# On-chip transposes for all 21 first slots and hardware-queue weight loads with a GpSimd cast, in a fused attention and feed-forward kernel

## The chip, the cores and the metric

The kernel runs on one core of a Trainium2 chip. The metric is device microseconds of one execution, in the median of several. All runs that are used here are fast. Sizes below about 2% are resolved by repeated rounds in which the kernel under test and the kernel before run on the same chip. A ratio is the mean time of one kernel's fast runs over that of the other's of the same rounds, so it isn't quite the ratio of the medians that are quoted beside it.

## The reference

Attention with a threshold, then a feed-forward layer, all in float32 on the outside:

```python
scores = (q @ k.T) / sqrt(64)                 # 8 batches, 8 heads, 576 tokens, 64 columns
scores = where(scores >= max(scores) - tau, scores, -1e9)
attn   = exp(scores - max(scores)); attn /= sum(attn) + 1e-9
x      = attn @ v                             # heads side by side: (4608, 512)
h      = x @ w_in                             # w_in (512, 2048)
out    = (h * clip(h + 3, 0, 6) / 6) @ w_out  # w_out (2048, 512)
```

## The kernel before

The attention is cut into 144 slots of two 128x576 score tiles each. In one iteration of the main loop the engines work on neighbouring slots: VectorE takes the maxima of slot n, ScalarE the exponentials of slot n-1 and the masks of slot n, TensorE the scores of slot n+1, GpSimd the normalization of slot n-1. GpSimd and SyncE take their instructions in program order in every trace read here (below, at 108.44 us, a small instruction stands behind a cast that waits).

The normalized tile must be transposed for the product with v. Slots up to 20 with an odd number are transposed on TensorE (nine 128x128 transposes into PSUM, one VectorE copy); all others by a DMA transpose that SyncE issues:

```python
sl.on_chip = len(queue) < N1 - 1 and len(queue) % 2 == 1        # N1 = 22
...
def sm_norm(sl):                                                # GpSimd
    for i in range(2):
        nc.gpsimd.tensor_scalar(out=pn[:, i, :], in0=sl.s[:, i, :], scalar1=sl.rinv[:, i:i + 1], ...)
    if not sl.on_chip:
        nc.sync.dma_start_transpose(out=sl.dst, in_=pn)
```

The feed-forward weights arrive as bf16 through 32 casting DMAs of 128x512, which the program issues from GpSimd (the prediction names why). The end of an iteration, which the change edits (cut):

```python
queue[n + 1].tiles = scores(...)       # TensorE
if n < 8:
    warm_up(6)                         # six float32 transposes of the identity, to no purpose but the clock
if prev is not None:
    sm_norm(prev)
flush(); late.extend(outs)
start(loads, 1)                        # q and k, SyncE
if n < 4 or n > 12:
    start(vcasts, 1)                   # v, a casting DMA from GpSimd
if n > 3:
    start(casts, 1 if n < 24 else 2)   # weights, casting DMAs from GpSimd
```

The first product with w_in comes in slot 23, the first with w_out in slot 31. From about there TensorE is the bound.

## Time and profile before

| | before |
|---|---|
| median of the first three runs | 562.35 us |
| profiled span | 562.3 us |
| TensorE, ScalarE, VectorE, GpSimd busy | 95%, 84%, 75%, 54% |
| mask of slots 0, 23 and 31 starts at | 10.7, 82.5 and 112.25 us |

The busy shares are means over two stages: up to slot 31 ScalarE and GpSimd lead, afterwards TensorE. The prediction shows the busy time by stretch. In the lines of a profile PE is TensorE, DVE VectorE, ACT ScalarE and POOL GpSimd; SPq and POOLq are what SyncE and GpSimd do to issue. What else one needs of the profile before are two lines of the page's part on DMA issues (destination and source, issuing queue, count, size, time from issue to landing), where the 32 weight DMAs stand:

```profile
w_in_sb<-in_moe_w_in_dram POOLq DMA_DIRECT2D x16, 128.0 KB, 4.1
w_out_sb<-in_moe_w_out_dram POOLq DMA_DIRECT2D x16, 128.0 KB, 4.5
```

Here are GpSimd and the mask that waits for it in the iteration of slot 28, from the instructions in order of time (start, duration, engine, line and operation, with the idle time before it in brackets):

```profile
98.92 0.80 POOL L121 DMA_DIRECT2D vm<-in_v_dram  x1
99.72 1.07 POOL L146 DMA_DIRECT2D w_out_sb<-in_moe_w_out_dram  x2
100.87 0.46 POOL L280 TENSOR_SCALAR bias<-m 128x1 f32<-128x1 f32 x2
101.08 1.44 ACT L285 ACTIVATE s<-s,bias 128x576 f32<-128x576 f32 x2 [1.39 <-POOL bias L280]
```

GpSimd spends 1.9 us on issuing a v load and two weight loads, and the tiny bias behind them makes ScalarE stand still for 1.39 us. Nobody waits for the data of these DMAs: their destinations lie fixed in memory and are needed slots later.

### The profile page before, as it was taken

To read this page: it belongs to the slowest core of one execution; us is meant where nothing else is said; L and a number is where in the kernel's file an instruction comes from. 1 tells how busy PE (TensorE), PEld (TensorE's weight loads), DVE (VectorE), ACT (ScalarE), POOL (GpSimd) and SP (SyncE) were. 2 spreads that over 40 slices of the span, in tenths; PEclk is the share of its full clock that TensorE was granted. 3 is DMA by queue.
4 is the path that set the end of the run, shared out by engine and by line. 5 is a ranking of instruction groups with operands and counts; after the bars stand their busy time and mean duration, and the time that the engine had idled before them with its cause. 6 is when DMAs were issued, how large, how long until landed. Compare 5 with 4: busy or idle time off the path is not lost.

```text
span 562.3 us, 11634 instructions
## 1 busy us (share of the span) xinstructions
PE 535.0 (95%) x3856; PEld 309.3 (55%) x3856; DVE 424.4 (75%) x1040; ACT 470.3 (84%) x999; POOL 305.2 (54%) x646
## 2 busy tenths in 40 slices
PE   7998798899999999999999999999999999999997
PEld 5665455455545565555555565655555565654663
DVE  3588787687878788787878798887978798883440
ACT  4799899798988999989898999899898999983540
POOL 1678878854556555655456555755556555561000
PEclk8899999899999999999999999999999999999999
DMA  5879999997689876978589867987699865453102
GB/s 110 135 110 166 162 160 184 207 148 144 112 159 153 151 153 127 208 139 155 114 150 170 159 137 146 174 160 146 127 137 175 167 124 117 101 109 86 38 20 75
DMA packets 286204, 77.52 MB, mean 138 GB/s; under 512 B 269248, under 2 KB 281536, under 8 KB 286144
## 3 DMA queue, kind: packets, MB, share of 16 engines
q1 hardware_dynamic: 268736, 67.86, 64.8%
q0 software_dynamic: 17408, 8.92, 13.7%
q8 instruction: 30, 0.49, 0.4%
q14 instruction: 30, 0.25, 0.2%
HBM read 36.70 MB, written 9.44 MB: 82 GB/s over the span
## 4 chain that ended last, share of the span: by engine, by line
PE 58%; DVE 11%; ACT 9%; issue 4%; POOL 1%; DMA 1%; SPq 1%; DVEq 0%; POOLq 0%
PE h L353 18%; PE o L382 17%; PE s L256 16%; DVE s L277 5%; ACT s L285 4%; PE av L323 3%; ACT s L290 3%; DVE g L370 2%; DVE r L364 2%; ACT r L362 2%; PE s L262 1%; PE tp L213 1%; PE ar L323 1%; DVE osb L390 1%; POOL pn L298 1%
## 5 line engine op out<-in xcount | busy, mean ns | idle before, releaser
L298 POOL TENSOR_SCALAR pn<-s,rinv 128x576 bf16<-128x576 f32 x288 | 211.6, 745 | 133.5 <-issue 58.5
L277 DVE TENSOR_SCALAR_CACHE_REDUCE s<-s 128x576 f32<-128x576 f32 x288 | 205.9, 752 | 44.9 <-PE s L256 35.2
L285 ACT ACTIVATE s<-s,bias 128x576 f32<-128x576 f32 x288 | 207.1, 766 | 36.8 <-POOL bias L280 35.7
L290 ACT ACTIVATE s<-s 128x576 f32<-128x576 f32 x288 | 192.7, 671 | 0.3
L256 PE MATMUL s<-kT,qT 64*128 64x288 f32 x1024 | 172.7, 435 | 5.4 <-DVE s L277 3.2
L353 PE MATMUL h<-xT,w_in_sb 128*128 128x320 bf16 (+1 forms) x1024 | 145.0, 287 | 5.5 <-DVE g L370 4.6
L382 PE MATMUL o<-w_out_sb,g 128*128 128x512 bf16 x576 | 140.9, 379 | 3.6 <-DVE osb L390 3.0
L353 PEld LDWEIGHTS <-w_in_sb 128*128 128x128 bf16 x1024 | 92.0, 97 | 68.4 <-issue 31.1
L256 PEld LDWEIGHTS s<-kT,qT 64*128 64x128 f32 x1024 | 94.8, 188 | 62.7 <-DVE s L277 24.9
L370 DVE SCALAR_TENSOR_TENSOR g<-r,h 128x512 bf16<-128x512 f32 (+1 forms) x128 | 96.4, 754 | 41.2 <-ACT r L362 39.3
L280 POOL TENSOR_SCALAR bias<-m 128x1 f32<-128x1 f32 x288 | 54.4, 189 | 69.0 <-DVE s L277 48.2
L382 PEld LDWEIGHTS <-g 128*128 128x128 bf16 x576 | 55.6, 98 | 58.2 <-issue 9.8
L362 ACT ACTIVATE r<-h,three 128x640 f32<-128x640 f32 (+1 forms) x74 | 54.4, 737 | 21.1 <-PE h L353 20.4
L290 ACT ACTIVATION_READ_ACCUMULATOR s<-s 128x1 f32 x288 | 54.2, 188 | 0.0
L364 DVE TENSOR_SCALAR r<-h 128x512 f32<-128x512 f32 (+1 forms) x54 | 40.5, 751 | 0.0
L390 DVE TENSOR_SCALAR osb<-o 128x512 f32<-128x512 f32 x31 | 21.0, 676 | 22.2 <-PE o L382 22.2
L323 PE MATMUL av<-pT,vm 128*64 128x512 bf16 x256 | 34.6, 392 | 2.0 <-ACT kT L203 2.0
L323 PEld LDWEIGHTS <-vm 128*64 128x64 bf16 x512 | 18.1, 111 | 25.2 <-issue 18.3
L293 DVE RECIPROCAL rinv<-rsum 128x2 f32<-128x2 f32 x144 | 23.0, 160 | 10.2 <-ACT s L290 9.5
L335 DVE CAST xT<-av 128x512 bf16<-128x512 f32 x32 | 21.8, 681 | 5.6 <-PE av L326 5.3
L277 DVE DVE_READ_ACCUMULATOR s<-s 128x1 f32 x288 | 23.9, 83 | 0.0
L388 ACT ACTIVATE osb<-o 128x512 f32<-128x512 f32 x5 | 3.0, 597 | 23.9 <-PE o L382 23.9
(42 smaller groups left out, 255.9 us busy)
## 6 DMA issues: line engine op xcount, KB each, us to landing
km<-in_k_dram SPq DMA_DIRECT2D x64, 128.0 KB, 3.0
out_dram<-osb SPq DMA_DIRECT2D x32, 256.0 KB, 2.4
nq<-in_q_dram SPq DMA_DIRECT2D x96, 72.0 KB, 2.7
vm<-in_v_dram POOLq DMA_DIRECT2D x16, 256.0 KB, 5.4
nq<-in_q_dram SPq DMA_DIRECT2D x16, 128.0 KB, 3.9
w_in_sb<-in_moe_w_in_dram POOLq DMA_DIRECT2D x16, 128.0 KB, 4.1
w_out_sb<-in_moe_w_out_dram POOLq DMA_DIRECT2D x16, 128.0 KB, 4.5
pT<-pn SPq DMA_TRANSPOSE x119, 3.4
```

Of the source, the lines that this page charges most:

```text
L256: nc.tensor.matmul(tiles[a][:, hf, 0:HALF], qT_of(pair)[a * 64:(a + 1) * 64, t * P:(t + 1) * P], keys(pair, a, hf), start=True, stop=True)
L277: nc.vector.tensor_scalar(out=sl.s[:, i, :].rearrange("p (a b) -> p a b", a=2), in0=ps[:, :, 0:HALF], scalar1=1.0, scalar2=None, op0=Alu.m ...
L280: nc.gpsimd.tensor_scalar(out=sl.bias[:, i:i + 1], in0=sl.m[:, i:i + 1], scalar1=-scale, scalar2=tau, op0=Alu.mult, op1=Alu.add)
L285: nc.scalar.activation(out=s, in_=s, func=Act.Prelu, bias=sl.bias[:, i:i + 1], scale=scale, alpha=REJECT)
L290: nc.scalar.activation(out=s, in_=s, func=Act.Exp, accum_out=sl.rsum[:, i:i + 1])
L298: nc.gpsimd.tensor_scalar(out=pn[:, i, :], in0=sl.s[:, i, :], scalar1=sl.rinv[:, i:i + 1], scalar2=1.0, op0=Alu.mult, op1=Alu.mult)
L323: nc.tensor.matmul(ps[a * 64:(a + 1) * 64, :], vm[:, 2 * hp + a, c * D:(c + 1) * D], pT[:, 5 * a + c, cols], start=(c == 0), stop=False)
L353: nc.tensor.matmul(hps[:, n, 0:w], w_in_sb[:, ki, (ni + n) * P:(ni + n + 1) * P], xT[b][:, ki, c0:c0 + w], start=(ki == 0), stop=(ki == KI ...
L362: nc.scalar.activation(out=r, in_=hps, func=Act.Relu, bias=three[:])
L364: nc.vector.tensor_scalar(out=r, in0=hps, scalar1=3.0, scalar2=0.0, op0=Alu.add, op1=Alu.max)
L370: nc.vector.scalar_tensor_tensor(out=gbuf[:, ni:ni + 2, c0:c0 + w], in0=r, scalar=6.0, in1=hps, op0=Alu.min, op1=Alu.mult)
L382: nc.tensor.matmul(o_ps[0], gbuf[:, ni, mt * P:(mt + 1) * P], w_out_sb[:, ni, :], start=(ni == 0), stop=(ni == NI - 1))
```

## The change

The intent: transposing all of the first 21 slots on TensorE takes eleven DMA transposes out of the busiest stage and keeps TensorE's clock up with useful work in place of warm-ups; loading the weights as float32 through SyncE's hardware queue frees GpSimd from issuing them and moves longer rows. GpSimd then casts from a staging buffer.

```diff
+    w_pool = ctx.enter_context(tc.tile_pool(name="wp", bufs=3))
...
+        def load(dst, src):
+            st = w_pool.tile([P, 2, 512], F32, tag="w", name="w")
+            nc.sync.dma_start(out=st[:], in_=src)
+            for n in range(2):
+                landed.append((dst[:, n, :], st[:, n, :]))
...  (16 loads of 512 KB in place of 32 casting DMAs)
+    def cast():
+        dst, src = landed.pop(0)
+        nc.gpsimd.tensor_copy(out=dst, in_=src)
...
-            sl.on_chip = len(queue) < N1 - 1 and len(queue) % 2 == 1
+            sl.on_chip = len(queue) < N1 - 1
...
-        if n < 8:
-            warm_up(6)
...
-        if n > 3:
-            start(casts, 1 if n < 24 else 2)
+        for _ in range(0 if n < 5 else 1 if n < 24 else 2):
+            if landed:
+                cast()
+        if n > 1 and len(landed) < 5:
+            start(wloads, 1)
```

("landed" is a list that the program keeps while it is built: what has been issued and not yet cast.)

More of the change, by code (lines that the diff above doesn't have):

```diff
@@ L74 @@
     loads = []
-    casts = []
+    wloads = []
     vcasts = []
@@ L137 @@
     w_out_sb = singles.tile([P, NI, d_model], BF16)
+    landed = []
     def load_weights():
-        for n4 in range(4):
-            for ki in range(KI):
-                casts.append(lambda n4=n4, ki=ki: nc.gpsimd.dma_start(
-                    out=w_in_sb[:, ki, n4 * 512:(n4 + 1) * 512],
-                    in_=moe_w_in[ki * P:(ki + 1) * P, n4 * 512:(n4 + 1) * 512]))
-        for ni in range(NI):
-            casts.append(lambda ni=ni: nc.gpsimd.dma_start(
-                out=w_out_sb[:, ni, :], in_=moe_w_out[ni * P:(ni + 1) * P, :]))
+        def load(dst, src):
[3 more added lines that the diff above has]
+                landed.append((dst[:, n, :], st[:, n, :]))
+        for n2 in range(2):
+            for ki in range(KI):
+                c = slice(n2 * 1024, (n2 + 1) * 1024)
+                wloads.append(lambda ki=ki, c=c: load(w_in_sb[:, ki, c].rearrange("p (n m) -> p n m", n=2),
+                                                      moe_w_in[ki * P:(ki + 1) * P, c].rearrange("p (n m) -> p n m", n=2)))
+        for ni in range(0, NI, 2):
+            wloads.append(lambda ni=ni: load(w_out_sb[:, ni:ni + 2, :],
+                                             moe_w_out[ni * P:(ni + 2) * P, :].rearrange("(n p) m -> p n m", n=2)))
+    def cast():
+        dst, src = landed.pop(0)
+        nc.gpsimd.tensor_copy(out=dst, in_=src)
     def start(jobs, n):
```

## The prediction

> **What bounds the kernel now.** I first read the page of the kernel before: the span, the busy shares and the costliest groups.
>
> ```profile
> span 562.3 us, 11634 instructions
> PE 535.0 (95%) x3856; PEld 309.3 (55%) x3856; DVE 424.4 (75%) x1040; ACT 470.3 (84%) x999; POOL 305.2 (54%) x646
> ```
>
> TensorE looks like the bound, but that is an average, and the change touches only the beginning: the 21 first slots and the weight loads, which end with slot 29. So the second view is the busy time by stretch, cut where the masks of slots 0, 5, 13, 17, 22 and 31 start, with the end of the slots at 507 us.
>
> ```profile
> core 0: us, PE busy (x) PEld busy (x) DVE busy (x) ACT busy (x) POOL busy (x), PEclk, DMA share, GB/s
> 10.72:28.33 17.61, 16.36 (x97) 10.78 (x97) 10.19 (x30) 14.00 (x30) 11.14 (x23) 0.81 0.76 126
> 28.33:51.43 23.10, 22.16 (x187) 13.56 (x184) 19.44 (x53) 22.07 (x49) 18.91 (x40) 1.00 0.85 123
> 51.43:64.69 13.26, 10.29 (x86) 5.54 (x80) 10.15 (x30) 11.09 (x25) 12.22 (x24) 1.00 1.42 192
> 64.69:79.11 14.42, 12.08 (x101) 6.96 (x98) 11.60 (x30) 13.64 (x30) 11.81 (x25) 1.00 1.10 160
> 79.11:112.25 33.14, 28.23 (x185) 17.54 (x185) 22.81 (x62) 28.59 (x63) 26.72 (x54) 0.95 1.23 185
> 112.25:507.00 394.75, 388.68 (x2871) 221.18 (x2870) 327.65 (x803) 360.00 (x776) 222.11 (x471) 1.00 0.81 145
> ```
>
> After 112 us TensorE is 98% busy and nothing of the change happens there. The change can therefore only move the moment at which slot 31 starts, and whatever it moves is carried unshortened to the end. Before 112 us the leaders are ScalarE (96% in 28 to 51 us) and GpSimd (92% in 51 to 65 us). In 11 to 18 us the TensorE clock was halved: read microsecond by microsecond, it is 0.50 from 11 to 17 us.
>
> The third view, the instructions in order of time, shows who makes whom wait there. Slots 9 to 10, with GpSimd and ScalarE alone:
>
> ```profile
> 40.91 1.47 POOL L298 TENSOR_SCALAR pn<-s,rinv 128x576 bf16<-128x576 f32 x2
> 42.32 0.58 POOL L142 DMA_DIRECT2D w_in_sb<-in_moe_w_in_dram  x1
> 42.98 0.46 POOL L280 TENSOR_SCALAR bias<-m 128x1 f32<-128x1 f32 x2
> 43.19 1.44 ACT L285 ACTIVATE s<-s,bias 128x576 f32<-128x576 f32 x2 [0.24 <-POOL bias L280]
> ```
>
> The mask of slot 10 waits for its bias; the bias waited for the weight DMA's issue, 0.58 us, on GpSimd; that waited for the normalization. GpSimd's cycle (two biases 0.46, normalization 1.47, one issue 0.58, gaps about 0.2) is 2.7 us, and ScalarE's own (mask 1.35, two exponentials 1.34, end to start) is 2.7 to 2.8. They are matched; slots 5 to 13 took 23.10 / 8 = 2.89 us each. Slots 13 to 17, whose iterations also issue v loads of 0.66 to 0.80 us, took 3.3: there GpSimd rules. Transfers are not in this chain: with a DMA share of 1.42 no long wait ends on one.
>
> **What the Trainium skill says.** "DMA: Bandwidth & Descriptors", section "SWDGE vs HWDGE vs iDMA": a DMA that casts can only be issued from GpSimd, whose cores build its descriptors; a plain one can go through SyncE. The trace agrees about the price on GpSimd: 0.58 us an issue. "GPSIMD Engine Reference", section "4.1 Engine selection": one-input elementwise work on GpSimd is roughly line-rate. The trace has the same kind: a normalization of 576 columns is 745 ns, one of 1 column 189 ns, so 0.97 ns a column. "TensorE: Matmul & The Clock Gate", Part 4 "PE-mode transpose": a transpose needs a copy out of PSUM, and it doesn't count as busy for the clock in the way a matmul does. On the first point the trace agrees (a copy of 0.75 us); on the second no view decides, as the warm-up transposes are always mixed with scores.
>
> **The change part by part.**
>
> *Weights.* Removed: 32 GpSimd issues of 0.56 to 0.58 us. Added: 32 GpSimd casts of 128x512. Estimate of one from the two durations above: 189 + 511 x 0.97 = 683 ns. Each is thus 0.1 us more than the issue it replaces, 3.2 us of GpSimd time in all. On the path: the iterations of slots 5 to 23 issue one; where GpSimd leads (four with v loads, about half of the rest) that is 0.1 x 4 + 0.1 x 7 = 1.1 us. Slots 24 to 29 have two, 1.35 us against 1.11. There, ScalarE waits for a bias behind the issues in four of six (0.56 and 1.39 us of waiting at 89.8 and 101.1 us are the clear ones), so 4 x 0.24 = 1.0 us. The last cast slides to slot 30; as todo2 first needs w_out at slot 31 nothing waits for it.
>
> SyncE gets 16 loads of 512 KB. A load must land before its cast, which is in GpSimd's fixed order before the next bias. Casts follow loads by four slots (12 us), but from slot 24 on by two (some 7 us), while SyncE is also issuing DMA transposes that take it 1.3 to 3.7 us each; loads of 128 KB land in 3.9 us. I give a late landing one chance in four and 3 us: +0.7 us.
>
> *Transposes.* Removed: 11 DMA transposes, off the path, so 0. Added: 11 times nine TensorE transposes (0.66 us a set at full clock) and 11 VectorE copies (0.75 us, 8.2 us in all). VectorE's cycle becomes: maxima 1.36, reciprocal 0.08, copy 0.65, and 0.57 on average of q, k and attention copies (5.15 us in nine slots) = 2.66 us, just below ScalarE's. Nearly hidden on average. It shows where an iteration that had no set before now has one beside the attention product of 1.4 us on TensorE, 0.66 + 1.43 + 1.24 (scores) = 3.3 us: slots 8 and 12, some 0.4 us each, +0.8 us.
>
> *Warm-ups.* Eight groups of six go (1.54 us at half clock, 0.87 at full). They delay the scores where TensorE is half-clocked:
>
> ```profile
> 13.35 1.54 PE L164 MATMUL warm<-identf 128*128 128x128 f32 x6
> 14.82 2.29 PE L256 MATMUL s<-kT,qT 64*128 64x288 f32 x8
> 17.14 0.76 DVE L277 TENSOR_SCALAR_CACHE_REDUCE s<-s 128x576 f32<-128x576 f32 x1 [2.84 <-PE s L256]
> ```
>
> Without the first group these scores end at the earliest when the maxima of slot 1 (14.22 us) free their banks, so about 0.7 us sooner; after that VectorE's copies and the normalization lead and the other groups are worth nothing. -0.7 us. Against it: the half clock may last one window more. At half clock a slot's TensorE work is 4 to 4.7 us, so it costs 1.5 us or more; one chance in three, +0.5 us.
>
> Sum: 1.1 + 1.0 + 0.7 + 0.8 - 0.7 + 0.5 = +3.4 us. I take off 1 us: waits overlap, so that the parts don't add fully, and fewer transfers at once can shorten SyncE's delays. 562.3 + 2.4 = 564.7, rounded to 564.5.
>
> **The rivals.**
>
> *Less traffic is worth something.* The DMA share is over 1 from 51 to 112 us, and eleven transposes and the casting transfers leave it. For: issues of transposes that took SyncE 8 to 10 us for two or three. Against: the only transfer wait that the table of waits shows in 9 to 80 us is far below its first ten rows, the shortest of which is 2.5 us. If it were true, 558 to 560 us.
>
> *All three cycles lock into one another.* With a set in each slot TensorE waits for the normalization each time (7.4 us over 14 weight loads now, every second slot), and scores stand behind the set in its queue. The loop: exponential end, reciprocal 0.2, normalization start 0.3 and 1.47, transposes 0.5, q or k transposes 0.6, scores 1 to 1.2, first maximum and bias 1.0 = 5.1 to 5.3 us, against two ScalarE slots, 5.5 us. It fits, with 0.3 us to spare; if it is 0.5 us longer, each of 21 slots gains 0.1 to 0.2 us: 567 us.
>
> *The clock stays low.* If transposes really don't count, TensorE might remain at half for ten slots at 1.5 us each: 575 to 580 us. Against: from slot 8 on there is no warm-up now and the clock holds at 1.00.
>
> *GpSimd's cast is slow.* At 1.2 us instead of 0.68, each of 32 casts adds 0.5 us more, mostly on the path: 575 us. The one-input rate measured by the normalization speaks against it.
>
> **Range and chances.** Each of the first two rivals is a matter of 4 us or less, so eight times in ten 560.0 to 570.0. A gain of over 2% would need 11 us, out of the some 100 us in which ScalarE is already 85 to 96% busy: 2%. A loss of over 2% needs one of the last two rivals: 6%. Within 2%: 92%.
>
> **What would show it.** Slot 31's mask starts near 114.5 us instead of 112.25, and the stretch from there to the end keeps its length. Casts are 0.65 to 0.70 us. Slots 5 to 13 take 2.9 to 3.1 us each, those with v loads 3.4. The clock is back at 1.00 by 18 us, or by 21.5. No wait of GpSimd for a weight load is above 1 us. Wrong would be: a cast far from 0.68 us, GpSimd waiting on loads in slots 24 to 30, a shift that arises after slot 31, or one that is negative because ScalarE's waits for biases shrink.

## The result, and the profile after

| | before | after |
|---|---|---|
| median | 562.73 us (4 runs, 562.04 to 564.07) | 567.28 us (4 runs, 566.87 to 568.96) |
| ratio | | 1.0084, 95% interval 1.0055 to 1.0112 |
| profiled span | 562.3 us | 565.6 us |

The change costs 0.8%. It is a clear loss, and within 2%. The page of the kernel after, span and busy shares:

```profile
span 565.6 us, 11706 instructions
PE 531.0 (94%) x3866; PEld 309.3 (55%) x3907; DVE 431.3 (76%) x1051; ACT 469.9 (83%) x999; POOL 308.1 (54%) x646
```

No total tells anything: GpSimd is 2.9 us busier, VectorE 6.9 us (it makes eleven copies more). The busy time by stretch does, cut at the masks of slots 0, 5, 13, 17, 26 and 31 (columns as in the prediction):

```profile
10.71:26.49 15.78, 12.96 (x86) 8.01 (x86) 11.28 (x31) 13.69 (x31) 10.63 (x22) 0.89 0.99 206
26.49:50.09 23.60, 21.70 (x204) 13.42 (x203) 21.69 (x58) 22.04 (x49) 19.30 (x40) 1.00 0.46 118
50.09:64.16 14.07, 10.59 (x96) 6.09 (x95) 11.85 (x34) 11.11 (x24) 12.57 (x24) 1.00 0.91 181
...
92.48:117.24 24.76, 17.13 (x126) 11.18 (x125) 14.26 (x38) 16.18 (x37) 17.45 (x33) 0.93 1.17 195
```

Of the kernel before, the last of these stretches (slots 26 to 31) is:

```profile
92.99:112.25 19.26, 15.03 (x93) 9.40 (x92) 12.43 (x32) 16.01 (x37) 16.17 (x32) 0.91 1.37 202
```

Length after minus length before: slots 0 to 5, 15.78 - 17.61 = -1.8 us; slots 5 to 13, +0.5; slots 13 to 17, +0.8; slots 26 to 31, 24.76 - 19.26 = +5.5 us, during which every engine is idler than before. Slots 17 to 26 add nothing. So slot 31 starts 5.0 us later; of this 0.8 us are made up by slot 35, and the profiled spans differ by 3.3 us.

What fills the 5.5 us? The instructions that touch the staging tile (duration in ns as smallest, median, largest; then the idle time that ended with each releaser, and how often):

```profile
L161 POOL CAST w_in_sb<-w x16: 610/614/624, 28.4 to 74.4; 128x512 bf16<-128x512 f32 x16
...
  DMA w<-in_moe_w_out_dram: 5.8, 4
```

A cast is 0.61 us, hardly more than the issue it replaces. But four casts waited 5.8 us in all for their data. In order of time, slots 29 and 30:

```profile
104.14 0.80 POOL L122 DMA_DIRECT2D vm<-in_v_dram  x1
...
104.95 0.62 POOL L161 CAST w_out_sb<-w 128x512 bf16<-128x512 f32 x1
...
107.74 0.61 POOL L161 CAST w_out_sb<-w 128x512 bf16<-128x512 f32 x1 [2.17 <-DMA w<-in_moe_w_out_dram]
108.44 0.46 POOL L294 TENSOR_SCALAR bias<-m 128x1 f32<-128x1 f32 x2
108.66 1.44 ACT L299 ACTIVATE s<-s,bias 128x576 f32<-128x576 f32 x2 [3.50 <-POOL bias L294]
```

The second cast of the iteration finds its load still under way, the bias stands behind it in GpSimd's queue, and ScalarE is idle for 3.5 us. The chain of work that ended last, which in the kernel before ran through engines here, now runs through the loads:

```profile
96.50 4.91 DMA w<-in_moe_w_out_dram
101.46 0.60 POOL w_out_sb L161
...
105.19 7.74 DMA w<-in_moe_w_out_dram
112.97 0.36 POOL w_out_sb L161
```

A load of 4.91 us and one of 7.74 us are on the path. What sent them out so late was SyncE's queue and no buffer. The load issued at 102.10 us takes the buffer of three loads earlier, whose last cast had ended at 94.96 us; but SyncE was busy with a transpose and four q loads from 97.17 to 102.01 us. Counted so, from the instructions in order of time, the four late loads were issued 2.1, 4.6, 3.5 and 6.5 us before GpSimd was ready to cast them, and took 4.0, 4.9, 5.6 and 7.7 us to land.

**The theory.** With three staging buffers of two casts each and two casts a slot from slot 24 on, a load precedes its cast by two slots, too little when SyncE issues it only after the slot's transposes and it lands in 4 to 8 us. (The number of buffers acts through the program: it limits how many loads may be written ahead of their casts.) This late landing is the main loss. Rivals: the TensorE transposes in each slot lock the engines together; GpSimd's casts cost the time in themselves; and, for the lateness itself, SyncE's order or the traffic rather than the buffers.

### The profile page after: what moved, and what is told of

Its sections match the earlier page's. It is cut to its first block, busy times and chain, and to the rows that moved or that the text cites. A ratio compares the mean times of both kernels' runs of the same rounds, so it can differ in the third digit from the quotient of the medians.

```text
span 565.6 us, 11706 instructions
## 1 busy us (share of the span) xinstructions
PE 531.0 (94%) x3866; PEld 309.3 (55%) x3907; DVE 431.3 (76%) x1051; ACT 469.9 (83%) x999; POOL 308.1 (54%) x646
## 4 chain that ended last, share of the span: by engine, by line
PE 59%; DVE 12%; ACT 7%; POOL 7%; DMA 5%; issue 3%; SPq 1%; DVEq 0%; POOLq 0%
PE o L396 17%; PE h L367 17%; PE s L270 16%; DVE s L291 5%; POOL pn L312 4%; PE av L337 4%; ACT s L299 3%; ACT s L304 2%; DVE g L384 2%; DMA w<-in_moe_w_out_dram 2%; DMA nq<-in_q_dram 2%; DVE r L378 2%; PE tp L227 1%; PE s L276 1%; ACT r L376 1%
## 5 line engine op out<-in xcount | busy, mean ns | idle before, releaser
L270 PE MATMUL s<-kT,qT 64*128 64x288 f32 x1024 | 170.2, 433 | 4.9 <-DVE s L291 2.1
L396 PE MATMUL o<-w_out_sb,g 128*128 128x512 bf16 x535 | 133.5, 379 | 5.6 <-DVE osb L404 2.7
L328 PE MATMUL pt<-identb,pn 128*128 128x128 bf16 x189 | 17.3, 225 | 6.4 <-POOL pn L312 6.3
```

The costliest lines, as they stand in the source:

```text
L270: nc.tensor.matmul(tiles[a][:, hf, 0:HALF], qT_of(pair)[a * 64:(a + 1) * 64, t * P:(t + 1) * P], keys(pair, a, hf), start=True, stop=True)
L396: nc.tensor.matmul(o_ps[0], gbuf[:, ni, mt * P:(mt + 1) * P], w_out_sb[:, ni, :], start=(ni == 0), stop=(ni == NI - 1))
```

## The experiments

**A measure for the clock.** Runs of one kernel differ by up to 5.5 us, and each run lists its mean granted clock. I fitted one line to 115 fast runs (71 of the experiments and the kernel after, 44 of the kernel before): a common slope and one offset for each kernel. The slope is 0.30 us for each 0.001 of clock; the residual is 0.75 us (standard deviation). "At equal clock" below is the difference of the offsets to the kernel before. It takes the lottery of the clock out, but also any part of the clock that a kernel brings on itself, so I give it beside the medians. The kernel after is +3.8 us at equal clock, +4.55 in the medians. The offsets have 95% intervals of 0.7 to 0.8 us either way.

**e1_early_loads.** A fourth buffer and the load written at the head of the iteration:

```diff
-    s_pool = ... bufs=4        +    s_pool = ... bufs=3        # room for the fourth staging buffer
-    w_pool = ... bufs=3        +    w_pool = ... bufs=4
-        if n > 1 and len(landed) < 5:  start(wloads, 1)        # end of the iteration
+        if n > 1 and len(landed) < 7:  start(wloads, 1)        # head of the iteration
```

> The changed kernel with a fourth staging buffer (the score buffers go from four to three to make room) and each weight load issued at the head of its slot, so that a load leads its cast by about four slots from slot 24 on, and not by two. Theory (late landing): the 5.8 us that GpSimd waits for weight loads between slots 26 and 30 fall below 1 us, and as they carry some 5 us of the loss, the time comes to 562 us (561 to 563.5), at or a little under the kernel before. Rival (GpSimd's casts themselves, or the TensorE transposes, cost the time): the casts and the transposes are all there, so it stays at 566 us or more.

Measured: 564.51 us (562.51 to 567.18, 6 runs), before 562.83; ratio 1.0027 (0.9999 to 1.0056); +1.8 us at equal clock. The waiting for loads fell to 1.3 us in one piece. Between the two expectations: the casts' lateness was worth some 2 us at equal clock, 2.8 us in the medians, and not all of the loss. What e6 showed later holds here too: the load's new place in the program changes almost nothing in SyncE's queue, so what acted was the fourth buffer and the higher limit that goes with it.

**e2_onchip_nowarm.** All 21 slots on TensorE and no warm-ups, weights as before:

```diff
-            sl.on_chip = len(queue) < N1 - 1 and len(queue) % 2 == 1
+            sl.on_chip = len(queue) < N1 - 1
-        if n < 8:
-            warm_up(6)
```

> The kernel before with all 21 first slots transposed on TensorE and the eight groups of warm-ups removed; the weights still come by casting DMAs from GpSimd. Theory: the start gains 1.9 us as in the changed kernel, slots 12 to 17 lose 0.5 to 1.2 us of it, nothing waits for loads: 561.5 us (560.5 to 562.5). Rival (transposes in each slot lock the engines): 564 us or more.

Measured: 562.68 us (561.32 to 564.72, 6 runs), before 562.83; ratio 0.9992 (0.9962 to 1.0021); +0.2 us at equal clock. This half of the change is worth nothing that these rounds resolve (0.65 us either way at equal clock). The rival of locked engines falls. The theory's gain of 1.3 us didn't come either; see e4.

**e3_weights_only.** The other half: the kernel after with

```diff
-            sl.on_chip = len(queue) < N1 - 1
+            sl.on_chip = len(queue) < N1 - 1 and len(queue) % 2 == 1
+        if n < 8:
+            warm_up(6)
```

> The changed kernel with every second slot transposed by DMA and the warm-ups put back: the weight path alone. Theory: nothing is gained at the start, and the late w_out loads cost 4 to 6 us between slots 26 and 31, minus about 1 us made up later: 566 to 569 us, with GpSimd waiting 4 us or more for weight loads. Rival (transposes cost the time): within 1 us of the kernel before.

Measured: 566.96 us (566.22 to 568.19, 6 runs), before 562.83; ratio 1.0073 (1.0050 to 1.0096); +3.7 us at equal clock. GpSimd waits 3.9 us for loads, in four places (4 or more were expected). The weight path alone carries the whole loss: at equal clock 3.7 + 0.2 = 3.9 us against 3.8 for both halves together.

**e4_nowarm_only.** The kernel before without its eight groups of warm-ups.

```diff
-        if n < 8:
-            warm_up(6)
```

> The kernel before without the eight groups of warm-ups, nothing else. Theory (the warm-ups delay the scores of the first slots): the mask of slot 5 starts 1.5 to 2 us earlier, and the time is 561 us (560.3 to 561.8). Rival (they keep TensorE's clock up): the half clock lasts longer than the 6 us of before, and the time is 563 us or more.

Measured: 562.76 us (561.58 to 564.65, 6 runs), before 562.83; ratio 1.0000 (0.9975 to 1.0025). At equal clock it is 1.1 us faster, but its mean clock is 0.9900 against 0.9950: 0.0050 x 0.30 us / 0.001 = 1.5 us. Both expectations may thus be true at once and cancel, that the warm-ups delay work and that they hold the clock; the second is not shown, as the mean clock of six runs has a standard error of 0.002. Neither time that was expected came, and in its profile the mask of slot 5 starts 0.9 us earlier (27.47 against 28.33), where 1.5 to 2 us were expected.

It also corrected me on the start. I had read the 1.9 us that the kernel after gains by slot 2 as the removal of the warm-ups. But e3, which keeps them, has the same gain in its profiled run (slot 2 at 16.29 us, against 18.23 before and 16.30 after). So where the clock is full the warm-ups cost nothing by slot 2. Where the half clock meets them they may: slot 2 starts 7.5 us after slot 0 in the two profiles that have all warm-ups and the half clock from about 11 us (before and e9; e8 has more issues on GpSimd there and is left out), and 5.6 us in e3 and in every profile without warm-ups. But no profile without them has the half clock so early, so the two are not separated. Two readings a microsecond wide (the third number from the right is the granted clock), of the kernel after,

```profile
13.00:14.00 1.00, 1.00 (x4) 0.50 (x5) 0.54 (x3) 1.00 (x3) 0.40 (x2) 0.76 0.64 40
17.00:18.00 1.00, 1.00 (x9) 0.73 (x9) 1.00 (x2) 1.00 (x3) 1.00 (x2) 1.00 0.92 233
```

and of e4:

```profile
20.00:21.00 1.00, 0.20 (x2) 0.20 (x4) 0.75 (x2) 1.00 (x2) 1.00 (x2) 0.94 1.27 261
27.00:28.00 1.00, 1.00 (x12) 1.00 (x12) 0.93 (x6) 0.56 (x2) 0.27 (x2) 0.64 1.02 226
```

The half clock lasts from 13.5 to 17.0 us in the first, from 20.9 to 27.7 in the second; it was 11.0 to 17.8 us in the kernel before and 60.8 to 64.2 us in e3. The lengths are one or two times 3.4 us and the place moves. A single profile says nothing about the start.

**e5_four_buffers.** Only the fourth staging buffer, for which one of the four score buffers makes room:

```diff
-    s_pool = ... bufs=4        +    s_pool = ... bufs=3
-    w_pool = ... bufs=3        +    w_pool = ... bufs=4
-        if n > 1 and len(landed) < 5:
+        if n > 1 and len(landed) < 7:
```

> The changed kernel with a fourth staging buffer (score buffers three), loads still issued at the end of their slot. If it is the lead of a load over its cast that is short: one slot more of lead cuts GpSimd's 5.8 us of waiting for weight loads to 1 to 3 us, and the time falls by 1 to 2.5 us against the changed kernel, to some 565 to 566 us. If it is SyncE's queue alone that holds the load back (its transposes stand before the load), buffers don't help: 5 us of waiting and 567 us.

Measured: 564.73 us (562.97 to 565.95, 4 runs), before 562.80; ratio 1.0033 (1.0009 to 1.0056); +1.5 us at equal clock. The staging tile's instructions between 80 and 122 us:

```profile
L161 POOL CAST w_out_sb<-w x15: 610/614/622, 82.2 to 113.6; 128x512 bf16<-128x512 f32 x15
...
  DMA w<-in_moe_w_out_dram: 1.0, 1
...
DMA to landing us min/median/max: 3.9/4.9/6.1
```

The casts take as long as before, and the loads land no sooner in the median (4.9 us in both; at most 7.7 in the kernel after, in the same stretch), yet the waiting fell from 5.8 to 1.0 us. It was the lead: the higher limit puts each of the last loads at least one iteration earlier into SyncE's queue. This recovers 2.3 us at equal clock (1.1 either way), 2.6 us in the medians. The missing score buffer costs nothing that the profiles show: slots 5 to 26 take 65.95 us here and 65.99 in the kernel after, and from slot 35 to the end it is 435.5 and 435.1 us.

**e6_issue_first.** Three buffers, the load at the head of the iteration:

```diff
+        if n > 1 and len(landed) < 5:          # ahead of load_quad(1) and the maxima
+            start(wloads, 1)
...
-        if n > 1 and len(landed) < 5:          # at the end
-            start(wloads, 1)
```

> The changed kernel with three buffers, but each weight load issued at the head of its slot, ahead of the slot's DMA transpose and q and k loads. If SyncE's order holds the loads back: waiting falls from 5.8 to 1 to 3 us, 565 to 566 us. If it is the number of buffers: the load waits for the cast that frees its buffer just as before, and waiting stays at 4 us or more, 567 us.

Measured: 567.92 us (566.90 to 570.78, 5 runs), before 562.80; ratio 1.0092 (1.0070 to 1.0114); +3.7 us at equal clock, and 5.5 us of waiting in four places: the kernel after once more. It had to be, and this was my mistake: nothing is issued between the end of one iteration and the head of the next. Set side by side, the instruction streams of SyncE differ only around the first three or four w_in loads and are the same from there on. So this run is a repeat of the kernel after, which serves to see how well a result repeats, and says nothing on SyncE's order.

**e7_no_transposes.** The first 31 slots on TensorE, no DMA transpose beside the last loads:

```diff
-            sl.on_chip = len(queue) < N1 - 1
+            sl.on_chip = len(queue) < 31
```

> The changed kernel with the first 31 slots transposed on TensorE, so that no DMA transpose runs beside the last five weight loads. If traffic of the transposes and their place in SyncE's queue make those loads late: the loads of slots 24 to 27 land in under 4.5 us, and GpSimd waits under 1.5 us for them. If only the lead of two slots is too short: waiting stays at 4 us or more. The time is open, as TensorE and VectorE get ten more sets in slots that have products as well: 564 to 570 us.

Measured: 580.67 us (576.82 to 581.36, 4 runs), before 562.80; ratio 1.0304 (1.0273 to 1.0335). For the question it was made for, the loads' landing between 80 and 122 us:

```profile
DMA to landing us min/median/max: 3.3/4.0/4.1
```

No cast waits at all, with three buffers, as was expected if the transposes make the loads late. But the run changes more than that. Its slots are so much longer (below) that the last four loads are issued 9.3 to 9.9 us before their casts, enough even for a landing of 7.7 us, and between the masks of slots 23 and 31 the DMA share is 0.54 in place of 1.10. So the loads do land sooner, in 4.0 us in the median against 4.9; whether that comes of the missing transposes alone, and whether it would have ended the waiting without the longer slots, is not shown. As a version it is bad, for another reason:

```profile
101.67 0.66 PE L328 MATMUL pt<-identb,pn 128*128 128x128 bf16 x9 [1.50 <-DVE g L384]
```

From slot 23 on the transposes and the first product of the feed-forward layer take turns in the one PSUM tile with the tag "h", and TensorE stands 1.5 us until VectorE has read the product out. Slots 24 to 32 take 4 to 7 us each.

**e8_issues_moved.** Not the change, but what it taught: the kernel before with the same casting DMAs, issued in other slots.

```diff
-        if n > 3:
-            start(casts, 1 if n < 24 else 2)
+        start(casts, 0 if n < 1 or 12 < n < 17 else 2 if n < 5 or n > 22 else 1)
```

> The kernel before with the same 32 casting DMAs issued at other slots: two each in slots 1 to 4, one in 5 to 12, none in 13 to 16 (where v loads are issued too), one in 17 to 22, two in 23 to 27, none from 28. If GpSimd's fixed order sets the path wherever v loads and weight issues meet, slots 13 to 16 shrink from 3.3 to about 2.8 us and the 1.4 and 1.1 us of ScalarE's waiting at slots 28 and 29 go: 2 to 4 us less, 559 to 561 us. If those slots are bound by the others anyway: within 1 us of before.

Measured: 560.68 us (559.66 to 561.06, 6 runs), before 562.80; ratio 0.9959 (0.9943 to 0.9976); 2.1 us less at equal clock. It beats both kernels. GpSimd in slots 13 to 15, and with the mask of slot 29:

```profile
53.41 0.80 POOL L121 DMA_DIRECT2D vm<-in_v_dram  x1
54.29 0.50 POOL L280 TENSOR_SCALAR bias<-m 128x1 f32<-128x1 f32 x2
...
101.63 0.80 POOL L121 DMA_DIRECT2D vm<-in_v_dram  x1
102.52 0.46 POOL L280 TENSOR_SCALAR bias<-m 128x1 f32<-128x1 f32 x2
102.73 1.44 ACT L285 ACTIVATE s<-s,bias 128x576 f32<-128x576 f32 x2
```

Where only a v load is issued, the bias follows it closely and the mask doesn't wait. Slots 13 to 17 take 11.26 us in place of 13.26. The wait at slot 28 is still there (1.26 us, the last two weight DMAs meet a v load in the iteration before), the one at slot 29 is gone.

**e9_weights_four.** e3 with the fourth buffer of e5.

> The weight path alone as in the run with warm-ups and alternate transposes, but with the fourth staging buffer. That run was 3.7 us over the kernel before at equal clock (a straight line through all runs' times and granted clocks). If the late loads are the whole of it but for the 0.05 us by which a cast is longer than an issue: at most 1 us of waiting for loads is left, and the time is 0.3 to 1.5 us over before at equal clock, 563 to 564.5 us. If a load through SyncE and a cast cost more than that by themselves: 2.5 us or more over before.

Measured: 565.04 us (562.51 to 567.49, 6 runs), before 561.83; ratio 1.0050 (1.0015 to 1.0084); +1.9 us at equal clock. One wait of 1.1 us is left. The buffer takes away half of the weight path's loss, as in e5; it lands between the two expectations, so a part of some 2 us (0.7 either way) is not late landing alone. The profile accounts for it loosely: slots 4 to 22 take 0.8 us more than before and slots 22 to 31 1.5 us more, of which the wait is 1.1, and 0.8 us come back by slot 35.

**e10_moved_two_less.** e8 without the warm-ups of slots 0 and 1:

```diff
-        if n < 8:
+        if 1 < n < 8:
```

> The kernel with the issues moved, with the first two groups of warm-ups left out, those that stand before the scores of slots 2 and 3 while TensorE may be at half clock. If the first groups only delay: 0.7 us less than the moved version, 560.0 us. If they help the clock come back: the mean granted clock falls below its 0.995, and the time is the same or up to 1 us more.

Measured: 560.36 us (559.72 to 561.21, 6 runs), before 561.83; ratio 0.9968 (0.9937 to 0.9998); 1.9 us less at equal clock, mean clock 0.9960. It can't be told from e8; the first two groups are worth nothing that these rounds resolve.

**e11_load_before_qk.** Three buffers, the load moved ahead of the q and k loads of the iteration. This was to be the test of SyncE's order that e6 was not:

```diff
         if prev is not None:
             sm_norm(prev)
+        if n > 1 and len(landed) < 5:
+            start(wloads, 1)
         flush(); late.extend(outs)
         start(loads, 1)
...
-        if n > 1 and len(landed) < 5:          # at the end
-            start(wloads, 1)
```

> The issue-first run moved the load past nothing but the slot's boundary: from the fourth load on SyncE's queue was the same as in the changed kernel, so it didn't test the order. This run does: three buffers, the load right behind the slot's DMA transpose and ahead of its q and k loads, which take SyncE up to 3.5 us; its buffer was freed by the casts of the slot before. If the order holds the loads back as well as the buffers: waiting for loads falls from 5.8 to 1 to 3 us and the time to about 565 us (1.5 to 2.5 us over before at equal clock). If only the number of buffers counts: 4 us of waiting or more, 567 us.

Measured: 570.24 us (569.79 to 572.72, 6 runs), before 562.65; ratio 1.0147 (1.0122 to 1.0172); +5.6 us at equal clock. What was expected missed: it is worse than the kernel after by 1.8 us at equal clock. SyncE's queue in order of time shows why, of the kernel after

```profile
92.91 0.55 SPq L146 DMA_DIRECT2D w<-in_moe_w_out_dram  x1
93.56 1.35 SPq L320 DMA_TRANSPOSE pT<-pn  x1
94.95 1.45 SPq L89 DMA_DIRECT2D km<-in_k_dram  x2
96.50 0.57 SPq L146 DMA_DIRECT2D w<-in_moe_w_out_dram  x1
```

and of this one:

```profile
94.20 1.33 SPq L320 DMA_TRANSPOSE pT<-pn  x1
95.58 0.58 SPq L146 DMA_DIRECT2D w<-in_moe_w_out_dram  x1
96.21 1.24 SPq L89 DMA_DIRECT2D km<-in_k_dram  x2
```

At the new place the count of what is not yet cast is taken before the slot's two casts, so it is higher, and the load is put off to the next iteration: behind that iteration's transpose, where it had stood ahead of it. Each of the last five loads is issued one transpose later. The waiting of GpSimd, between 80 and 126 us, rises from 5.8 to

```profile
  DMA w<-in_moe_w_out_dram: 8.5, 5
```

So the move I meant as earlier was a later one, and shows the effect with the other sign: one transpose later costs 2.7 us of waiting and that 1.8 us. The place in SyncE's queue counts.

**e12_both.** The same move with four buffers. It was meant to bring the load earlier; against e5 it comes later, as will be seen:

```diff
-    s_pool = ... bufs=4        +    s_pool = ... bufs=3
-    w_pool = ... bufs=3        +    w_pool = ... bufs=4
+        if n > 1 and len(landed) < 7:          # behind sm_norm(prev), in place of the end
+            start(wloads, 1)
```

> The same with the fourth staging buffer. The last 1.0 to 1.1 us of waiting for loads should go (under 0.3 us left), which leaves what the weight path costs without any late landing: 0.5 to 1.5 us over before at equal clock, 563.5 to 564.5 us. If it stays at 1.9 us or more over before, the loss outside late landing is not in this wait.

Measured: 566.00 us (564.25 to 567.81, 6 runs), before 562.65; ratio 1.0061 (1.0038 to 1.0084); +3.1 us at equal clock, 1.6 us worse than e5 with the same buffers. It was to be the version without any late landing, and it isn't one: GpSimd still stands idle before two casts, for 2.0 and 1.6 us.

```profile
  DMA nq<-in_q_dram: 2.0, 1
  DVE rinv L307: 1.6, 1
```

The profile puts these waits down to a q load and to a reciprocal, neither of which a cast reads. In order of time one finds what held the first:

```profile
97.99 0.58 SPq L146 DMA_DIRECT2D w<-in_moe_w_out_dram  x1
...
105.01 0.61 POOL L161 CAST w_out_sb<-w 128x512 bf16<-128x512 f32 x1 [1.98 <-DMA nq<-in_q_dram]
```

This is the last load but one, and its cast. The staging tile's view of the stretch 97.9 to 98.6 us gives its landing as 7.0 us, so at 105.0 us; the last load, issued at 106.07 us, took 4.5 us, and its cast starts at 110.61. Both waits are for weight loads, 3.6 us in all. The reason is that of e11: the count is taken before the slot's casts, so each of the last loads is issued one transpose later than in e5. The move costs 1.6 us here and 1.8 us with three buffers (1.0 either way in both). The question of the run, what the weight path costs when no load is late, stays open.

## Why the prediction was right or wrong

The prediction said 564.5 us, in 560 to 570, within 2% of before. It came to 567.28 us: inside the range, the class right, the forecast loss of 2.2 us about half of the 4.55 us between the two medians. One of its own signs of being wrong came: GpSimd waited for weight loads, four times and up to 2.17 us, where no wait above 1 us was to be.

- **Bound: right; carrying of the shift: nearly.** The change acts before slot 31 (mask at 117.2 us, 5.0 us late, where 114.5 was expected). It was to be carried unshortened; in the profiles 3.3 us of it arrive at the end.
- **Cast against issue: right.** 0.61 us instead of the estimated 0.68, 0.05 us over the issue. The slots with v loads (13 to 17) take 3.43 us each in e3, which has the weights alone, against 3.32 before (13.26 / 4): the 0.1 that was predicted. In the kernel after they take 3.52. The two-cast slots cost less than the 1.0 us given to them: in e9, where the lateness is mostly gone, slots 22 to 29 are 0.3 us longer than before.
- **Late landing: the step that was mis-sized.** The prediction gave it "one chance in four and 3 us: +0.7 us". It happened in every profile with three buffers and transposes beside the loads (after, e3, e6, e11), as 3.9 to 8.5 us of GpSimd waiting. What the fourth buffer takes away is worth 567.28 - 564.73 = 2.6 us in the medians (after against e5; 2.3 at equal clock) and 566.96 - 565.04 = 1.9 us (e3 against e9, from different rounds; 1.8 at equal clock). With 2.6 in place of 0.7 the sum would have been 564.5 + 1.9 = 566.4 us, 0.9 from the measured time. That it comes so near is partly luck, as smaller terms missed in both directions. The working set a lead of some 7 us against a landing of 3.9 us, that of a 128-KB load. The four late loads of 512 KB took 4.0 to 7.7 us, and their lead was 2.1 to 6.5 us, because each was issued only when SyncE had come to it behind transposes and q or k loads.
- **Transposes: right in sum.** The prediction expected almost nothing (+0.8 us); at equal clock e2 less e4 gives 0.2 + 1.1 = 1.3 us (0.9 either way). Its place was half right: slots 12 to 17 lost 1.2 us in the kernel after and 0.9 us in e2, slot 8 nothing.
- **Warm-ups: the gain of 0.7 us has no place in the medians.** e4 shows 1.1 us gained at equal clock and about as much lost by the clock.
- **The rivals.** Less traffic gained nothing (e2 for the transposes; with the casting DMAs gone too, the whole change lost). The engines didn't lock (e2). The clock didn't stay low for ten slots. The cast was not slow. Half of the weight path's loss, the 1.9 us at equal clock that e9 keeps, is outside the waiting that a buffer removes; about 0.8 us of slots made longer by the casts and one last wait of 1.1 us are what the profile shows in its place. e12 was to separate them and didn't, as its loads were late.
- **On the lateness itself**, the theory named the buffers first. The runs show two things that set it: how many iterations ahead the program may write a load, which the buffers limit (e5, e9), and the load's place in SyncE's queue (e11, e12). That transposes beside the loads slow them is likely, but not separated (e7).

## What to carry to other kernels

Here a DMA that casts on its way cost GpSimd its issue, 0.56 to 0.58 us, and nobody waited for its data; a plain load with a cast behind it put a wait into the middle of an engine that works in order. Such a wait must be given a lead, counted from where the load comes out of its queue and not from where the program writes it, against the slowest landing of that size beside the traffic of that stage. When one engine's queue carries the small instruction that everybody waits for, look at what is issued before it, slot by slot: moving issues to slots with slack gained 0.4%, where replacing them lost 0.8%. When a wait is put down to something that the waiting instruction doesn't read, compare its start with the landings (e12). And read the start of a kernel from several runs with their clocks, not from one profile.

## What the Trainium skill lacked or had wrong

- "TensorE: Matmul & The Clock Gate", Part 1, says that the half clock comes in free-running windows of about 3.4 us and that this is run-variable. The runs agree (stretches of 3.4 and 6.8 us, at 11, 13.5, 20.9 or 60.8 us). It adds that the ramp penalty is under 1% of a typical kernel's span, and advises against fitting to one count of slow matmuls. The size agrees: the mean clock of the kernel before ranges from 0.988 to 1.000, at 0.30 us for 0.001 some 3.6 us or 0.6%. What the page lacks is that effects of 1 us can be read among such runs by a fit of time to mean clock.
- The same page, Part 4, has it that transposes don't count as busy for the clock as matmuls do. The runs don't settle it: without warm-ups the mean clock is 0.9900 (six runs of e4); with the same code and TensorE transposes in each of 21 slots it is 0.9947 (six of e2), and with the warm-ups, which are transposes themselves, 0.9950 (44 runs of before). But each mean of six has a standard error of 0.002.
- "GPSIMD Engine Reference", section 4.1, calls one-input work roughly line-rate but has no figure for a cast. A float32 to bf16 cast of 128x512 is 0.61 us here.
- "DMA: Bandwidth & Descriptors", section "DMA Transpose (X-bar)", says nothing on what ordinary loads beside transposes suffer. Between 80 and 122 us a 512-KB load landed in 4.0 us in the median (4.1 at most) in e7, without transposes but in longer slots, and in 4.9 us (7.7 at most) in the kernel after, with them. Transposes aren't the only cause: in the kernel after, whose first DMA transpose is issued at 80.8 us, the load issued at 17.6 us took 9.1 us, 2.2 of them in the issue itself.
